# Moving the decay guard's loads and sums one expert block later in an RWKV and mixture-of-experts kernel

## The chip, the cores and the metric

The kernel runs on one core of one Trainium2 chip. The metric is the device time of one execution in microseconds (us); the time of a version is the median of several executions. The engines are named as in the profile: PE is TensorE (PEld its weight loads), DVE is VectorE, ACT is ScalarE, POOL is GpSimd, SP is the queue that issues most DMA transfers. "L483" is line 483 of the kernel before.

## What is computed

An RWKV attention (4 batches, 8 heads, 768 steps, head size 48) feeds a mixture of 8 experts with top-1 routing (3072 tokens of width 384, hidden width 1024).

```python
for t in range(S):                                   # attention, per batch and head
    cur = einsum('bhd,bhe->bhde', u[None] * kt, vt)
    y[:, :, t] = einsum('bhd,bhde->bhe', rt, state + cur)
    state = wt[:, :, :, None] * state + einsum('bhd,bhe->bhde', kt, vt)
logits = x @ w_gate + modality_bias[modality_id]     # x = y, one row of 384 per token
e_idx = argmax(logits); gate_w = softmax(logits)[e_idx]
for e in range(E):                                   # experts
    h = maximum(x[mask] @ w1[e], 0.0)
    out[mask] = gate_w[mask, None] * (h @ w2[e])
```

The kernel's fast attention is written for decays `w` between 0.78 and 1.25. A "decay guard" reads all of `w` once more and sums by how much any element lies outside; if the sum is not zero, a slow general path (`any_decay`) runs at the end.

## The kernel before, in words

The attention stage and the routing come first (to about 122 us). Rows of tokens are then scattered to DRAM by expert, and seven expert blocks follow, `seq` = 0 to 6, of 512, 512, 384, 384, 384, 512 and 416 rows (`WIDTH`). The schedule is written by hand: each engine executes in the order in which the program emits its instructions.

A block has two stages. The up stage "u" has 8 steps (`blk_up`): in each PE makes 9 matmuls into one PSUM tile (L792), ACT takes the ReLU to `hh` (L796), and DVE makes the remainder `hl` (L797). The down stage "d" goes over row chunks j of 128 rows (4 chunks in a block of 512 rows), 4 steps for each chunk (`blk_down`, L813, 6 matmuls a step), so step s belongs to chunk s // 4. A chunk's sum stands in PSUM tile pY for even j and in pX for odd j. After a chunk, `blk_out` lets ACT copy it out as `ot` (L834), and POOL sends it off (L835). Blocks 2 to 5 convert the next block's rows (`blk_t`: DVE L770 and L778, ACT L776) ahead of the down stage, and split the next block's first weights (`w_split`: ACT L276, DVE or POOL L277) in the four steps of chunk 0.

Extra work is hung on a step with `at(block, stage, step, fn)`. Several functions on one step run in the order in which they were registered. The ones that matter here:

- `guard_load(n)` (L476 to L478), n = 0 to 7: SP issues the load of one eighth of `w` (128 x 1152 f32, 0.59 MB) into a `wg` tile. There are two `wg` buffers, so load n waits for the sums of n - 2.
- `guard(n)` (L480 to L484): two ReLU activations on ACT over that tile, each with an accumulator that goes to its own column of `gacc`.
- `flags()` (L693 to L710), in two parts, registered after the guard (L1003 to L1005) on steps 7 and 9 of the down stage of block 5. Part one: DVE reduces all 16 columns of `gacc` (L697) and compares with zero into `gb` (L698). Part two: PE multiplies `gb` with ones (L701, one column), and DVE makes the four flags from it (L703 to L709).
- At the start of block 6 every engine's sequencer loads the flags (L1010), which decide over the extra paths after the last block.

In the kernel before, the guard's loads hang on up steps 2 and 6 of blocks 1 to 4, and its sums on down steps 4 and 7 of the same blocks. The tags "wg" also serve two tiles of block 6 (`ht`, `st`).

Of the kernel before, what the change touches and what calls it, by code (L numbers as in the profile page):

```python
# [55 lines left out]
NG = 8  # L56
# [17 lines left out]
def kernel(ctx: ExitStack, tc: tile.TileContext, rkw, vt, wf, cst, mid, wg, bias, w1, w2, out):  # L74
# [867 lines left out]
    seq = [*range(NQ)]  # L942
# [11 lines left out]
    def at(q, ph, step, *fn):  # L954
        aux.setdefault((q, ph, step), []).extend(fn)
# [36 lines left out]
        at(q1, "u", e // 2, part(pad_rows, e))  # L992
    at(q1, "u", 4, part(blk_raw, seq[2], 0))
    at(q1, "d", 0, part(blk_load, seq[2]))
    for k, q in enumerate(seq[1:1 + NG // 2]):
        for n, ph, step in ((2 * k, "u", 2), (2 * k + 1, "u", 6)):
            at(q, ph, step, part(guard_load, n))
        for n, step in ((2 * k, 4), (2 * k + 1, 7)):
            at(q, "d", step, part(guard, n))
# [223 lines left out]
```

## Time and profile before

| what | us |
|---|---|
| median of 3 executions (334.73 to 335.19) | 335.15 |
| the profiled execution, own time | 335.87 |
| span in the trace of that execution | 334.1 |
| PE busy in the span | 323.0 (97%) |
| ACT busy | 206.2 (62%) |
| DVE busy | 238.4 (71%) |
| POOL busy | 158.8 (48%) |

The time around the span (335.87 less 334.1) is start and end that the trace doesn't cover. In the trace the down stage of block 1 runs from about 174.5 to 191.2 us, block 4 ends at about 266.7, the up stage of block 5 goes to 283.5, its down stage to 300.4, and block 6 to about 328.3, after which the last rows are written out. Times in rows are from the start of the span.

### The profile page before, as it was taken

The numbers are of one execution on the slowest core, as the hardware profiler recorded it, in microseconds if no ns is written. First come the engines' busy times: TensorE is split into PE (matmuls) and PEld (weight loads), VectorE is DVE, ScalarE is ACT, GpSimd is POOL, SyncE is SP. The second block draws the span as 40 slices with busy tenths as digits, with TensorE's granted clock in tenths as the row PEclk, the third lists the DMA queues.
The fourth block names the chain that finished last, engine by engine and source line by source line (L and its number), as shares of the span: only waits on it lengthen the run. The fifth ranks groups of instructions, "written<-read, shape, count | busy, mean of one in ns | idle before, by whom it ended". The sixth has DMA issues, their size and how long they took to land.

```text
span 334.1 us, 10250 instructions
## 1 busy us (share of the span) xinstructions
PE 323.0 (97%) x3915; PEld 298.8 (89%) x3915; DVE 238.4 (71%) x510; ACT 206.2 (62%) x516; POOL 158.8 (48%) x194
## 2 busy tenths in 40 slices
PE   8989899999999999999999999999999999999993
PEld 3779899999898988899889999999999988999982
DVE  7899999999999886696458858858358445815510
ACT  2478388688879994461449556956956944614420
POOL 5889999999999179136751210210220220121021
PEclk9999799999999999999999999999999999999999
DMA  7998888888894601614964800440560663210001
GB/s 220 404 307 249 248 257 267 263 261 268 264 312 154 145 4 47 144 71 169 301 195 120 254 32 0 108 177 2 114 194 2 197 141 96 94 72 22 0 32 55
DMA packets 38735, 52.31 MB, mean 157 GB/s; under 512 B 19189, under 2 KB 26133, under 8 KB 38676
## 3 DMA queue, kind: packets, MB, share of 16 engines
q1 hardware_dynamic: 35572, 42.09, 42.9%
q0 software_dynamic: 3104, 9.47, 7.6%
q8 instruction: 33, 0.54, 0.7%
q14 instruction: 26, 0.21, 0.2%
HBM read 55.43 MB, written 11.88 MB: 202 GB/s over the span
## 4 chain that ended last, share of the span: by engine, by line
issue 40%; PE 20%; POOL 8%; POOLq 2%; ACT 1%; DVE 0%; ACTq 0%
PE pS_u L792 6%; POOL out L835 6%; PE pY_d L813 3%; PE pX_d L813 2%; POOL xs L724 2%; PE pY L466 2%; POOLq L1032 2%; PE pS L415 1%; PE pY L455 1%; PE pR_x L520 1%; PE pU L435 1%; PE pR_x L321 1%; ACT dV L356 0%; POOLq L835 0%; POOLq L1010 0%
## 5 line engine op out<-in xcount | busy, mean ns | idle before, releaser
L835 POOL DMA_INDIRECT out<-ot,xg x25 | 27.4, 1096 | 132.7 <-ACT ot L834 130.6
L797 DVE SCALAR_TENSOR_TENSOR hl<-pS_u,hh 128x512 fp32r<-128x512 f32 (+2 forms) x56 | 34.6, 619 | 62.5 <-ACT hh L796 62.3
L792 PE MATMUL pS_u<-xh,wh 128*128 128x512 f32 (+2 forms) x168 | 61.6, 367 | 0.0
L796 ACT ACTIVATE hh<-pS_u 128x512 fp32r<-128x512 f32 (+2 forms) x56 | 30.3, 541 | 50.5 <-PE pS_u L792 50.5
L792 PE MATMUL pS_u<-xh,wl 128*128 128x512 f32 (+2 forms) x168 | 61.3, 365 | 0.0
L277 DVE TENSOR_TENSOR wl<-raw,wh 128x768 fp32r<-128x768 f32 x52 | 48.8, 962 | 2.3 <-ACT wh L276 1.9
L276 ACT CAST wh<-raw 128x768 fp32r<-128x768 f32 (+1 forms) x60 | 44.9, 786 | 0.0
L792 PE MATMUL pS_u<-xo,wh 128*128 128x512 f32 (+2 forms) x168 | 43.3, 365 | 0.0
L813 PE MATMUL pY_d<-wh,hh 128*128 128x384 f32 x112 | 37.8, 337 | 0.0
L813 PE MATMUL pY_d<-wh,hl 128*128 128x384 f32 x112 | 37.6, 336 | 0.0
L813 PE MATMUL pY_d<-wl,hh 128*128 128x384 f32 x112 | 37.6, 336 | 0.0
L724 POOL DMA_INDIRECT xs<-xp,posT x24 | 26.4, 1101 | 21.7 <-DVE posT L607 17.8
L335 DVE TENSOR_TENSOR_SCAN pX_s<-pw,pX_s 128x268 f32<-128x268 f32 x48 | 34.1, 711 | 1.0 <-POOL pw L282 0.7
L792 PEld LDWEIGHTS pS_u<-xh,wh 128*128 128x128 f32 x168 | 31.5, 188 | 3.2
L792 PEld LDWEIGHTS pS_u<-xh,wl 128*128 128x128 f32 x168 | 31.5, 188 | 3.1
L792 PEld LDWEIGHTS pS_u<-xo,wh 128*128 128x128 f32 x168 | 31.0, 188 | 3.6 <-DVE xo L778 0.3
L287 POOL TENSOR_TENSOR G<-in 128x512 f32<-128x512 f32 x24 | 31.1, 1294 | 4.7 <-DMA in<-rkw 4.7
L417 DVE TENSOR_TENSOR A<-pS,cs 128x1024 f32<-128x1024 f32 x24 | 29.2, 1218 | 1.0 <-PE pS L415 1.0
L415 PE MATMUL pS<-R,K 64*128 64x128 f32 x384 | 27.7, 285 | 2.2 <-DVE A L417 1.4
L356 ACT ACTIVATE dV<-v,dT 128x48 f32<-128x48 f32 x120 | 29.7, 328 | 0.0
L299 POOL TENSOR_TENSOR in<-in 128x512 f32<-128x512 f32 (+1 forms) x23 | 28.1, 1223 | 0.6
L415 PEld LDWEIGHTS pS<-R,K 64*128 64x128 f32 x384 | 24.2, 194 | 3.7 <-DVE A L417 2.2
(319 smaller groups left out, 672.5 us busy)
## 6 DMA issues: line engine op xcount, KB each, us to landing
raw<-w SPq DMA_DIRECT2D x24, 768.0 KB
in<-rkw SPq DMA_DIRECT2D x66, 256.0 KB
v<-vt SPq DMA_DIRECT2D x24, 192.0 KB
wg<-wf SPq DMA_DIRECT2D x8, 576.0 KB
raw<-w SPq DMA_DIRECT2D x16, 192.0 KB
xs<-zt SPq DMA_DIRECT2D x12, 193.0 KB
xq<-xs SPq DMA_DIRECT2D x12, 192.0 KB
xq<-xs SPq DMA_DIRECT2D x12, 144.0 KB
```

The lines of the kernel that those rows point to most:

```text
L276: nc.scalar.copy(out=wh[k][:, sl], in_=raw[k][:, sl])
L277: (eng or (nc.vector, nc.gpsimd)[k]).tensor_tensor(out=wl[k][:, sl], in0=raw[k][:, sl], in1=wh[k][:, sl].bitcast(F32), op=ALU.subtract)
L287: nc.gpsimd.tensor_tensor(out=G, in0=t[:, 0:512], in1=t[:, 512:1024], op=ALU.mult)
L335: nc.vector.tensor_tensor_scan(out=BE[:, ::step], data0=pp[:, ::step], data1=d1[:, ::step], initial=0.0, op0=ALU.mult, op1=ALU.max)
L356: nc.scalar.activation(out=dV[:, h], in_=v0[:, h], func=AF.Copy, scale=dT[:, h:h + 1])
L415: nc.tensor.matmul(out=pS[:, hh, p], lhsT=K[q, p], rhs=R[q, p], start=True, stop=True)
L724: rows_apart("xs", nc.gpsimd.indirect_dma_start(out=xs[:, :], out_offset=bass.IndirectOffsetOnAxis(ap=posT[:, n:n + 1], axis=0), in_=T["xb ...
L792: nc.tensor.matmul(out=pp, lhsT=wsrc[0][:, g, c * P:(c + 1) * P], rhs=xsrc[:, c, 0:w], start=(n == 0), stop=(n == 3 * KC - 1))
L796: nc.scalar.activation(out=hh, in_=pp, func=AF.Relu)
L797: nc.vector.scalar_tensor_tensor(out=hl, in0=pp, scalar=0.0, in1=hh.bitcast(F32), op0=ALU.max, op1=ALU.subtract)
L813: nc.tensor.matmul(out=X["y", q, j][0:r1 - r0], lhsT=hsrc[:, r0:r1], rhs=wsrc[1][:, f], start=(f == 0 and n == 0), stop=(f == FC - 1 and n ...
L835: ins = nc.gpsimd.indirect_dma_start(out=out[:, :], out_offset=bass.IndirectOffsetOnAxis(ap=xg[0:m, j, 1:2].bitcast(I32), axis=0), in_=ot[ ...
```

## The change

The guard's pairs of loads and sums move one block later: parts 0 and 1 from block 1 to block 2, 2 and 3 from block 2 to 3, 4 and 5 from block 3 to 4, 6 and 7 from block 4 to 5. The steps inside the block, the order of the parts and everything else stay.

```diff
@@ -992,7 +992,7 @@
     at(q1, "u", 4, part(blk_raw, seq[2], 0))
     at(q1, "d", 0, part(blk_load, seq[2]))
-    for k, q in enumerate(seq[1:1 + NG // 2]):
+    for k, q in enumerate(seq[2:2 + NG // 2]):
         for n, ph, step in ((2 * k, "u", 2), (2 * k + 1, "u", 6)):
             at(q, ph, step, part(guard_load, n))
         for n, step in ((2 * k, 4), (2 * k + 1, 7)):
             at(q, "d", step, part(guard, n))
```

## Rows read from the trace of the kernel before

**Rows 1.** The page: PE's busy time, and its granted clock in 40 slices.
```profile
PE 323.0 (97%) x3915; PEld 298.8 (89%) x3915; DVE 238.4 (71%) x510; ACT 206.2 (62%) x516; POOL 158.8 (48%) x194
...
PEclk9999799999999999999999999999999999999999
```
**Rows 2.** Waits of PE, whole run: us in total, times, longest.
```profile
PE pS L415 <- DVE A L417: 1.4, 2, 1.3
...
PE pU L435 <- ACT KT L401: 0.2, 1, 0.2
```
**Rows 3.** Busy time by stage: length, PE, PEld, DVE, ACT, POOL, clock, DMA, GB/s.
```profile
157.00:174.50 17.50, 17.50 (x78) 14.26 (x77) 8.45 (x18) 7.66 (x12) 11.86 (x12) 1.00 0.81 260
174.50:191.20 16.70, 16.70 (x98) 16.66 (x97) 14.67 (x57) 11.88 (x19) 4.47 (x4) 1.00 0.63 169
...
266.60:283.50 16.90, 16.90 (x75) 13.66 (x74) 8.16 (x11) 8.30 (x15) 1.96 (x2) 1.00 0.53 131
283.50:300.40 16.90, 16.90 (x100) 16.70 (x99) 8.83 (x21) 6.71 (x11) 3.50 (x3) 1.00 0.23 82
```
**Rows 4.** Timeline of SP: start, us, line, transfer; guard loads and their neighbours.
```profile
160.46 0.35 SPq L478 DMA_DIRECT2D wg<-wf  x1
...
185.93 0.91 SPq L478 DMA_DIRECT2D wg<-wf  x2
...
267.52 2.51 SPq L758 DMA_DIRECT2D xg<-xs  x1
275.64 8.74 SPq L271 DMA_DIRECT2D raw<-w  x2
```
**Rows 5.** Timeline of ACT, down stage of block 4.
```profile
260.92 0.57 ACT L834 ACTIVATE ot<-pY_d,xg 128x384 f32<-128x384 f32 x1
261.39 1.25 ACT L483 ACTIVATE jk<-wg,glo 128x1152 bf16<-128x1152 f32 x1
...
266.69 0.18 ACT L484 ACTIVATION_READ_ACCUMULATOR jk<-wg,ghi 128x1 f32 x1
266.78 0.56 ACT L834 ACTIVATE ot<-pX_d,xg 128x384 f32<-128x384 f32 x1
```
**Rows 6.** Timeline of ACT, down stage of block 5.
```profile
287.11 3.03 ACT L276 CAST wh<-raw 128x768 fp32r<-128x768 f32 x4
290.05 0.57 ACT L834 ACTIVATE ot<-pY_d,xg 128x384 f32<-128x384 f32 x1
292.12 0.58 ACT L834 ACTIVATE ot<-pX_d,xg 128x384 f32<-128x384 f32 x1 [1.50 <-PE pX_d L813]
```
**Rows 7.** Timeline of DVE, down stage of block 5, first part of the flags.
```profile
291.50 0.17 DVE L697 TENSOR_REDUCE gsf<-gacc 128x1 f32<-128x16 f32 x1
291.70 0.16 DVE L698 TENSOR_SCALAR gbf<-gsf 128x1 bf16<-128x1 f32 x1
```
**Rows 8.** Timeline of PE, down stage of block 5, chunks 2 and 3.
```profile
294.01 0.18 PE L701 MATMUL pU_g<-gbf,onesb 128*128 128x1 bf16 x1
294.05 0.42 PE L813 MATMUL pY_d<-wh,hh 128*128 128x384 f32 x1
...
296.21 0.34 PE L813 MATMUL pX_d<-wh,hh 128*128 128x384 f32 x1
```
**Rows 9.** Chain that ended last: start, us, what; DVE hands over to PE.
```profile
89.91 0.48 DVE xp L490
...
90.43 0.88 PE pY L455 x16
```
**Rows 10.** Stretches with a fallen clock (columns as Rows 3).
```profile
36.00:38.00 2.00, 1.17 (x18) 1.08 (x19) 1.78 (x3) 0.00 (x0) 1.85 (x5) 0.67 0.93 267
38.00:40.00 2.00, 2.00 (x26) 2.00 (x28) 1.97 (x6) 0.97 (x2) 2.00 (x3) 0.50 0.68 213
```
**Rows 11.** Timeline of PE, two waits in the attention stage.
```profile
18.43 1.16 PE L415 MATMUL pS<-R,K 64*128 64x128 f32 x16 [1.25 <-DVE A L417]
...
36.83 1.10 PE L466 MATMUL pY<-v,A 128*64 128x48 f32 x16 [0.97 <-issue]
```

## The prediction

> **What bounds the kernel now.** I read the page first, then PE's waits, then the stretches by stage, then the timelines of ACT, DVE, SP and PE where the moved work leaves and where it arrives. The page has PE busy 97% of the span at a granted clock of nine tenths or more in every slice but one [rows 1]. The list of PE's waits holds seven lines; each names a matmul of the attention stage (the first and the last stand in [rows 2]), and none a matmul of the expert blocks (L792, L813). The stretches agree: PE is busy 17.50 of 17.50 us in the up stage of block 1, 16.70 of 16.70 in its down stage, and 16.90 of 16.90 in both stages of block 5 [rows 3]. So from about 122 us on the time is PE's own work, without a gap, and then a short tail in which the last rows are written. A move of work on other engines can give nothing there. It can only cost, if it makes PE wait; and what PE loses in block 5 nothing later gives back, because block 6 is gapless too.
>
> **What the change removes: block 1.** Two loads go from SP (issued at 160.46 and some 6 us later) and four activations from ACT. The nearest stretches bound the gain: PE already has 17.50 of 17.50 and 16.70 of 16.70 us there [rows 3], so it is 0, although DMA engines are busy 0.81 of the up stage and will be less so. The loss is 0 too: nothing is added there.
>
> **What stays as it was: blocks 2 to 4.** Each still has two loads and two guards on the same steps, only other eighths of `w`. SP runs ahead of the other engines: a pair that hangs on the up stage of block 2 is already issued at 185.93, in the down stage of block 1 [rows 4] (one of three such pairs). Its order against the other transfers in these blocks stays. Cost 0.
>
> **What the change adds: block 5, loads.** SP has the last transfer of block 6's rows at 267.52, which takes it 2.51 us, and its next one only at 275.64 [rows 4]. The two loads of parts 6 and 7 fall into this hole, at about 270. Their buffers are free by then, since the sums of parts 4 and 5 end in block 4 at 266.87 [rows 5]. They move 2 x 0.59 = 1.18 MB. At the mean of that stretch, 131 GB/s at a DMA share of 0.53 [rows 3], that takes 9.0 us, and at the same rate with the engines full 131 / 0.53 = 247 GB/s, 4.8 us. So the data is there between 275 and 279, more than 11 us ahead of its use at 290.5 (below). The second weights of block 6, which SP issues from 275.64 to 284.4, come up to 4 us later at worst; their first use is in the up stage of block 6, after 300.4. Cost of the loads 0; their cover is these 11 and 16 us.
>
> **Block 5, sums, and the wait that they make.** This is where it costs. In block 4 ACT copies out chunk 0 at 260.92, starts the first of the four activations 0.47 us later, and the last accumulator is read at 266.69 + 0.18 = 266.87 [rows 5], thus 5.95 us after the start of `ot`. The four run back to back, though they hang on steps 4 and 7: ACT has nothing between them. In block 5 ACT comes to the same `ot` at 290.05, late, because it has just cast weights from 287.11 on without a pause [rows 6]; nothing of that is touched by the change. With the guard behind it the last sum is written at 290.05 + 5.95 = 296.00.
>
> Part one of the flags hangs on step 7 of this same stage, behind guard part 7. Its reduction reads all 16 columns of `gacc`, so it now waits for 296.00; before, it ran at 291.50 without a wait, when the sums had been done since block 4. A hand-over between engines takes about 0.04 us, by DVE at 89.91 + 0.48 = 90.39 and PE at 90.43 [rows 9]; I take the same, as an estimate, for ACT to DVE, with 0 and 0.10 as ends. The two DVE instructions take 291.70 + 0.16 - 291.50 = 0.36 us [rows 7]. So `gb` is ready at 296.00 + 0.04 + 0.36 = 296.40, and PE may start the flags' matmul at 296.44. PE comes to it at 294.01 [rows 8]. It executes in order, and the rest of chunk 2, chunk 3 and block 6 are queued behind that one-column matmul. PE waits 296.44 - 294.01 = 2.43 us. DVE's own wait, from about 291.5 to 296.0, holds up only the flags: DVE has no other work until block 6's first `hl`.
>
> Two smaller things. After the wait the next matmul may have to show its weight load: 0 to 0.2 us. I take 0, because the matmul behind L701 follows it after 0.04 us now [rows 8]. And ACT's `ot` of chunk 1, now at 292.12, moves to 290.05 + (266.78 - 260.92) = 295.91 and ends 0.56 later, at 296.47. Chunk 3 writes the same PSUM tile, at 296.21 now [rows 6, 8]; by itself that would be a wait of 0.30 us. But PE, late by 2.43, comes to chunk 3 at 298.64, and the wait vanishes in the larger one. What is late next is the flags themselves: ready 2.4 us later, like all of PE's work, so the loads of the flags at block 6 keep their distance.
>
> **The sum.** 0 + 0 + 0 + 2.43 = 2.43 us, with ends 2.35 and 2.75 from the hand-overs and the weight load. For the profiled execution: span 334.1 + 2.4 = 336.5, own time 335.87 + 2.43 = 338.30. That execution is 0.72 us above the median of the runs shown, so for the median 335.15 + 2.43 = 337.58.
>
> **Rival 1: the clock falls in the wait as well.** In the attention stage PE waited 0.97 us before 36.83 [rows 11]; around it the granted clock went from 1.00 (2.4 GHz) to 0.50 (1.2 GHz) and stayed there until about 40: 0.67 as the mean of one stretch of 2 us (1.3 us at half), and 0.50 in the whole next one [rows 10], 3.3 us together. After a longer wait, 1.25 us before 18.43 [rows 11], the slice shows nine tenths or more [rows 1]. So a wait alone doesn't decide it; before both of them PE had run short, narrow matmuls with gaps, while in block 5 it runs wide ones without any. For the fall speaks that 2.43 us is twice the longest wait that this trace has. Its price: 3.3 us at half clock in a stage of gapless work loses up to 1.65 us; with the fall inside the wait a part of that is free. Time 337.58 + 1.65 = 339.23.
> The Trainium skill, page "TensorE: Matmul & The Clock Gate", section "HAM oscillation — how this bites in real kernels", says that a TensorE left idle too long between bursts is taken back to half clock and starts the next burst cold. By that rule this change pays twice for its wait, 339.2 in place of 337.6; the trace has one wait that agrees and one that doesn't, so it stays a rival with its own chance.
>
> **Rival 2, not slower: ACT is through in time.** One mechanism, in one place: if ACT reached chunk 0's `ot` in block 5 early enough, the sums would end before PE needs `gb`. The point: 294.01 - 0.44 - 5.95 = 287.62 in place of 290.05. Against it: until 290.05 ACT is in the weight casts that begin at 287.11 [rows 6], and the change takes no work from ACT in block 5. For it: only that the order could differ from what I read, or that the flags' reduction didn't wait for the last sums. The change would then not do what its step list says (the guard on step 7 ahead of the flags on step 7). Then the 0.30 us at chunk 3 is all that is left, or nothing: 335.15 to 335.45, no change that can be told.
>
> **Rival 3: the loads come late.** If parts 6 and 7 landed after 290.5, the wait would grow one for one. That needs a landing over 20 us after the issue; 1.18 MB need 4.8 to 9.0. I give it as 340 or more.
>
> **How the numbers follow.** Forecast (wait of 2.4 us, clock kept): 0.58, 337.6. Rival 1: 0.30, 339.2. Rival 2: 0.08, 335.15 to 335.45. Rival 3 and anything else: 0.04, half of it slower, half of it a gain that I don't see. A measurement of this kernel can tell about 0.2% (0.7 us) from no change. Faster by more: 0.02; within: 0.08; slower by more: 0.90. The range takes in the forecast with its ends (337.5 to 337.9, and 0.4 below for what the runs of before scatter, 334.73 to 335.19) and rival 1 with the same scatter: 337.1 to 339.5.
>
> **What would show it.** In the profile of the changed kernel PE's waits should hold one new line, the flags' matmul (L701) behind DVE L698, of about 2.4 us; DVE should wait for ACT L484 ahead of L697, some 4.5 us; ACT should run `ot`, four activations and the next `ot` without a pause from 290.05; the down stage of block 1 should be as long as now, 16.7 us. Rival 1 would show as a granted clock of 0.50 for some 3 us after the wait, with matmuls of chunk 2 or 3 twice as far apart. The prediction is wrong if L701 starts with no wait, if ACT pauses ahead of the first activation in block 5 (the loads were late), or if any stage of blocks 1 to 4 gets shorter by more than 0.1 us.

## The result, and the profile after

The changed kernel takes 338.94 us (median of 338.66 to 339.48) against 335.17 us before (334.73 to 335.43): 3.77 us more, ratio 1.0118 with a 95% interval of 1.0102 to 1.0134. The forecast was 337.6 in a range of 337.1 to 339.5. Executions more than 1.5% above the fastest of the same kernel are left out of ratios and counts; that is one, of the kernel before.

In the changed kernel's waits of PE there is one new line, and it is the first of them (columns as in [rows 2]):

```profile
PE pU_g L701 <- DVE gbf L698: 2.3, 1, 2.3
PE pS L415 <- DVE A L417: 2.1, 4, 1.3
```

The timeline of ACT in the down stage of block 5 answers [rows 5, 6]:

```profile
288.62 0.57 ACT L834 ACTIVATE ot<-pY_d,xg 128x384 f32<-128x384 f32 x1
289.10 1.24 ACT L483 ACTIVATE jk<-wg,glo 128x1152 bf16<-128x1152 f32 x1
...
294.38 0.19 ACT L484 ACTIVATION_READ_ACCUMULATOR jk<-wg,ghi 128x1 f32 x1
294.48 0.56 ACT L834 ACTIVATE ot<-pX_d,xg 128x384 f32<-128x384 f32 x1
```

and that of DVE [rows 7]:

```profile
294.60 0.17 DVE L697 TENSOR_REDUCE gsf<-gacc 128x1 f32<-128x16 f32 x1 [4.45 <-ACT jk L484]
294.81 0.16 DVE L698 TENSOR_SCALAR gbf<-gsf 128x1 bf16<-128x1 f32 x1
```

ACT copies out chunk 0, runs the four activations without a pause, and DVE stands 4.45 us ahead of L697 until the last sum is there. PE, from the flags' matmul to block 6 (answers [rows 8]):

```profile
295.02 0.18 PE L701 MATMUL pU_g<-gbf,onesb 128*128 128x1 bf16 x1 [2.28 <-DVE gbf L698]
295.06 0.42 PE L813 MATMUL pY_d<-wh,hh 128*128 128x384 f32 x1
...
296.44 0.52 PE L813 MATMUL pY_d<-wh,hh 128*128 128x384 f32 x1
296.76 0.52 PE L813 MATMUL pY_d<-wl,hh 128*128 128x384 f32 x1
...
300.00 0.33 PE L813 MATMUL pX_d<-wl,hh 128*128 128x384 f32 x1
300.17 0.34 PE L813 MATMUL pX_d<-wh,hl 128*128 128x384 f32 x1
...
302.95 0.35 PE L792 MATMUL pS_u<-xh,wh 128*128 128x416 f32 x1
```

The wait is read best against ACT's copy of chunk 0 (`ot`), whose place in the stage no kernel here changes: L701 started 294.01 - 290.05 = 3.96 us after it before [rows 6, 8], and 295.02 - 288.62 = 6.40 us now. PE lost 2.44 us. Then it lost more: between 296.4 and 299 the matmuls are 0.32 us apart, before and after that 0.17. The granted clock says why (columns as in [rows 3]):

```profile
295.50:296.00 0.50, 0.50 (x4) 0.50 (x4) 0.43 (x5) 0.00 (x0) 0.50 (x1) 0.87 0.00 0
296.00:296.50 0.50, 0.50 (x4) 0.50 (x3) 0.26 (x2) 0.00 (x0) 0.29 (x1) 0.50 0.00 0
...
299.00:299.50 0.50, 0.50 (x4) 0.50 (x4) 0.00 (x0) 0.18 (x1) 0.04 (x1) 0.72 0.00 0
299.50:300.00 0.50, 0.50 (x4) 0.50 (x3) 0.00 (x0) 0.00 (x0) 0.50 (x1) 1.00 0.07 16
```

It fell to 0.50 (1.2 GHz) at about 295.9, 0.9 us after PE had begun again, and rose at about 299.3. From L701 to block 6 PE took 302.95 - 295.02 = 7.93 us. A profile of the same kernel without the fall has 6.36 (below), and so has the kernel before, 300.37 - 294.01. The fall cost 1.57 us. Wait and fall together are 4.01 us: from the copy of chunk 0 to block 6 it was 300.37 - 290.05 = 10.32 in the trace of before, whose line is

```profile
300.37 0.35 PE L792 MATMUL pS_u<-xh,wh 128*128 128x416 f32 x1
```

and is 302.95 - 288.62 = 14.33 now.

The span grew by only 336.8 - 334.1 = 2.7. In the execution that was profiled before, the clock fell in the attention stage [rows 10]; in this one it did not. Its blocks begin 1.4 us earlier (L792 first at 120.4 in place of 121.8); 0.4 us of this was there ahead of the fall:

```profile
36.00:38.00 2.00, 2.00 (x52) 1.88 (x51) 1.77 (x6) 0.97 (x2) 1.85 (x5) 1.00 0.92 306
```

4.01 - 1.43 = 2.58, and 0.1 in block 6, make up the 2.7. The rest is as forecast. There is no gap in block 1 (stretches, columns as in [rows 3]):

```profile
157.00:174.50 17.50, 17.50 (x78) 14.31 (x78) 9.18 (x19) 8.02 (x14) 12.15 (x11) 1.00 0.49 176
174.50:191.20 16.70, 16.70 (x98) 16.70 (x97) 13.93 (x56) 6.49 (x11) 3.35 (x4) 1.00 0.66 190
```

From the start of block 1 to the down stage of block 5 PE took the same in both, 283.60 - 157.79 = 125.81 us in the trace of before,

```profile
157.79 0.39 PE L792 MATMUL pS_u<-xh,wh 128*128 128x512 f32 x1
...
283.60 0.33 PE L813 MATMUL pY_d<-wh,hh 128*128 128x384 f32 x1
```

and 282.18 - 156.37 = 125.81 in that of the changed kernel:

```profile
156.37 0.39 PE L792 MATMUL pS_u<-xh,wh 128*128 128x512 f32 x1
...
282.18 0.33 PE L813 MATMUL pY_d<-wh,hh 128*128 128x384 f32 x1
```

And in the timeline of SP the loads of parts 6 and 7 stand in its hole, 20 us ahead of their use [rows 4]:

```profile
268.78 0.85 SPq L478 DMA_DIRECT2D wg<-wf  x2
274.21 8.74 SPq L271 DMA_DIRECT2D raw<-w  x2
```

### The profile page after: what moved, and what is told of

It reads as the page before. It is cut to its first block, busy times and chain, and to the rows that moved or that the text cites. A ratio compares the mean times of both kernels' runs of the same rounds, so it can differ in the third digit from the quotient of the medians.

```text
span 336.8 us, 10250 instructions
## 1 busy us (share of the span) xinstructions
PE 323.9 (96%) x3915; PEld 299.2 (89%) x3915; DVE 238.2 (71%) x510; ACT 206.3 (61%) x516; POOL 158.9 (47%) x194
## 4 chain that ended last, share of the span: by engine, by line
issue 41%; PE 20%; POOL 8%; POOLq 2%; ACT 1%; DVE 0%; ACTq 0%
PE pS_u L792 6%; POOL out L835 6%; PE pY_d L813 3%; PE pX_d L813 2%; POOL xs L724 2%; PE pY L466 2%; POOLq L1032 2%; PE pS L415 1%; PE pY L455 1%; PE pR_x L520 1%; PE pU L435 1%; PE pR_x L321 1%; ACT dV L356 0%; POOLq L835 0%; POOLq L1010 0%
## 5 line engine op out<-in xcount | busy, mean ns | idle before, releaser
L792 PE MATMUL pS_u<-xh,wh 128*128 128x512 f32 (+2 forms) x168 | 61.6, 367 | 0.0
L792 PE MATMUL pS_u<-xh,wl 128*128 128x512 f32 (+2 forms) x168 | 61.3, 365 | 0.0
L792 PE MATMUL pS_u<-xo,wh 128*128 128x512 f32 (+2 forms) x168 | 43.3, 366 | 0.0
L792 PEld LDWEIGHTS pS_u<-xh,wl 128*128 128x128 f32 x168 | 31.5, 188 | 3.2
L792 PEld LDWEIGHTS pS_u<-xh,wh 128*128 128x128 f32 x168 | 31.5, 188 | 3.2
L792 PEld LDWEIGHTS pS_u<-xo,wh 128*128 128x128 f32 x168 | 31.0, 188 | 3.6 <-DVE xo L778 0.3
L813 PE MATMUL pX_d<-wh,hh 128*128 128x384 f32 x80 | 27.2, 340 | 0.0
```

The lines of the kernel that those rows point to most:

```text
L792: nc.tensor.matmul(out=pp, lhsT=wsrc[0][:, g, c * P:(c + 1) * P], rhs=xsrc[:, c, 0:w], start=(n == 0), stop=(n == 3 * KC - 1))
L813: nc.tensor.matmul(out=X["y", q, j][0:r1 - r0], lhsT=hsrc[:, r0:r1], rhs=wsrc[1][:, f], start=(f == 0 and n == 0), stop=(f == FC - 1 and n ...
```

## The experiments

They ran on three other chips, four kernels on each, beside the kernel before. The chip of the result is called A here, the others B, C and D. There the executions of the kernel before scatter more (335.4 to 337.5 on B) than on A (334.7 to 335.4), so the intervals are wide, and the timelines carry most of the argument. "Above before" is the difference of the medians; the ratio, to which the interval belongs, is not that of the medians (on C, 3.87 us above before go with a ratio of 1.0101, which is 3.4 us).

**Theory:** PE waits 2.44 us at the flags' matmul for the last sums, and in some executions the clock falls in that wait. **Rival A:** the loads and sums in block 5 themselves slow it. **Rival B:** the move costs something in blocks 1 to 4.

### The flags later

```diff
-    at(seq[-2], "d", 7, part(next, fl))
-    at(seq[-2], "d", 9, part(next, fl))
+    at(seq[-2], "d", 10, part(next, fl))
+    at(seq[-2], "d", 12, part(next, fl))
```

> The changed kernel, with the two parts of the flags moved from steps 7 and 9 to steps 10 and 12 of block 5's down stage; the guard stays in blocks 2 to 5. Theory (PE waits at the flags' matmul for the last sums, and the clock falls in that wait): no wait at L701, no fall, 335.2 to 335.5; of the wait of 0.30 us at the first matmul of chunk 3, behind ACT's copy of chunk 1, now something is seen. Rival A (the loads and sums themselves slow block 5, by traffic or a busy ACT): still 337 or more. Rival B (the parts of the move in blocks 1 to 4 cost something): 336 or more. A new cost is possible: the flags end some 3 us later, 1.5 us ahead of block 6, and the sequencers' loads of them could hold up PE there by up to 1 us.

Measured on B: 337.45 against 335.99, 1.46 above before, ratio 1.0037 (1.0020 to 1.0053). That is more than the theory's 0 to 0.3 us, less than the 1.8 or more of Rival A, and within the 0.8 or more of Rival B. In the timeline of PE L701 starts without a wait, and the hidden wait behind ACT's copy of chunk 1 stands where the prediction had it:

```profile
296.24 0.44 PE L813 MATMUL pX_d<-wh,hh 128*128 128x384 f32 x1 [0.29 <-ACT ot L834]
...
297.39 0.18 PE L701 MATMUL pU_g<-gbf,onesb 128*128 128x1 bf16 x1
...
300.46 0.34 PE L813 MATMUL pX_d<-wh,hl 128*128 128x384 f32 x1
300.74 0.43 PE L792 MATMUL pS_u<-xh,wh 128*128 128x416 f32 x1
```

At block 6 PE is 0.1 us late (0.28 from start to start, where 0.17 is usual). From ACT's copy of chunk 0 (289.76) to block 6 it took 300.74 - 289.76 = 10.98 us, 0.66 more than the 10.32 of before, in place of 4.01 more. So the guard in block 5 costs 0.66 us here once the flags don't wait, and Rival A has the smaller part. The timed 1.46 us is more than that. The up stage of block 6 takes 0.2 us longer than in the trace of before, and that of block 1 0.6 us (17.39 against 16.80), the subject of the last experiment.

### Only the last pair in block 5

```diff
-    for k, q in enumerate(seq[2:2 + NG // 2]):
+    for k, q in enumerate((*seq[1:NG // 2], seq[-2])):
```

> The changed kernel, but only the last pair of parts (6 and 7) is in block 5; the others are in blocks 1, 2 and 3 as before the change, and block 4 has none. Theory: the whole cost comes from the last pair, so the time is that of the changed kernel, 338.9, with a wait of 2.4 us at L701. Rival B (the move in blocks 1 to 4 costs or gains something): it differs from 338.9 by more than 0.5 us.

Measured on B: 339.31, 3.3 above before, ratio 1.0100 (1.0064 to 1.0137). The timeline of PE has the whole wait:

```profile
296.12 0.18 PE L701 MATMUL pU_g<-gbf,onesb 128*128 128x1 bf16 x1 [2.35 <-DVE gbf L698]
```

One of the four pairs brings the whole wait: from ACT's copy to block 6 it is 12.76 us, 2.44 more than before. Against Rival B. But the clock did not fall here, and the mean granted clock is 0.993 to 0.995 in all four executions. The 0.9 us that are left of the 3.3 are then not a fall in the wait.

### The flags' matmul one, two and minus one steps later

```diff
-    at(seq[-2], "d", 9, part(next, fl))
+    at(seq[-2], "d", 10, part(next, fl))
```

In the other two the new step is 11 and 8.

> The changed kernel, with the second part of the flags (the matmul on PE) on step 10 in place of 9. PE comes to it one step of 1.04 us later, so the wait is 2.44 - 1.04 = 1.40 us. Theory: 335.2 + 1.4 = 336.6 if the clock stays, 338.1 if it falls all the same; which of them, the theory leaves open. Rival A (the loads and sums themselves): no change from 338.9.

> The changed kernel, with the second part of the flags on step 11. PE comes two steps of 1.04 us later: the wait is 2.44 - 2.08 = 0.36 us, the same length as the wait for ACT's copy at the first matmul of chunk 3, which comes right behind and is then covered. Theory: 0.3 to 0.5 us above the kernel before, no fall of the clock. Rival A (the loads and sums in block 5 themselves cost the time): 2 us or more above it.

> The changed kernel, with the second part of the flags (the matmul on PE) on step 8 in place of 9. PE comes to it one step of 1.04 us earlier, so the wait is 2.44 + 1.04 = 3.48 us. Theory: 1.04 us slower than the changed kernel, and the clock, after the longer wait, falls in at least as many executions: 4.6 to 5.1 us above the kernel before. Rival (not the wait): as the changed kernel.

| step of L701, chip | wait of PE there, by the sum | idle in the trace | copy of chunk 0 to block 6, longer by | above before, us | ratio, interval |
|---|---|---|---|---|---|
| 11, D | 0.36 | 0.22 | 0.42 | 0.56 | 1.0022 (1.0007 to 1.0038) |
| 10, B | 1.40 | 1.26 | 1.41 | 1.64 | 1.0034 (1.0010 to 1.0057) |
| 9 (the change), A | 2.44 | 2.28 | 4.01, with a fall | 3.77 | 1.0118 (1.0102 to 1.0134) |
| 9 (the change), D | 2.44 | 2.29 | 2.45, no fall | 3.49 | 1.0124 (1.0096 to 1.0153) |
| 8, D | 3.48 | 3.32 | 6.01, with a fall | 5.62 | 1.0173 (1.0140 to 1.0205) |

The trace counts idle time from the modelled end of the matmul before, so it shows 0.16 us less than the starts do. Loads, sums and their places are the same in all these kernels; only PE's arrival moves. In each profile L701 starts 6.40 us after ACT's copy of chunk 0 (6.41 in that with step 11): the sums are ready at one time, and PE waits for as long as it comes too early. The time follows it; for the longer two it rises by more than the wait. With step 8 it lies outside the 4.6 to 5.1 us expected: 2.13 us above the changed kernel beside it in place of 1.04. The timeline of PE in the kernel with step 8 shows the other part:

```profile
297.63 0.18 PE L701 MATMUL pU_g<-gbf,onesb 128*128 128x1 bf16 x1 [3.32 <-DVE gbf L698]
...
298.14 0.52 PE L813 MATMUL pY_d<-wl,hh 128*128 128x384 f32 x1
298.46 0.52 PE L813 MATMUL pY_d<-wh,hl 128*128 128x384 f32 x1
```

and so do its stretches (columns as in [rows 3]):

```profile
295.00:297.00 2.00, 0.00 (x0) 0.00 (x0) 0.00 (x0) 1.97 (x4) 0.00 (x0) 0.84 0.00 0
297.00:299.00 2.00, 1.37 (x5) 1.37 (x6) 1.25 (x9) 0.65 (x3) 0.98 (x1) 0.50 0.00 0
299.00:301.00 2.00, 2.00 (x7) 2.00 (x7) 0.00 (x0) 0.00 (x0) 0.00 (x0) 0.50 0.27 98
301.00:303.00 2.00, 2.00 (x8) 2.00 (x8) 0.00 (x0) 0.00 (x0) 0.00 (x0) 0.50 0.01 4
303.00:305.00 2.00, 2.00 (x13) 2.00 (x12) 0.00 (x0) 0.58 (x1) 0.54 (x1) 0.96 0.01 4
```

Here the clock falls while PE still waits, and stays at 0.50 until 303.2, twice as long as in the changed kernel on A.

### The wait filled

```diff
     pG = pt("g", "pU")
+    for _ in range(10):
+        nc.tensor.matmul(out=pG[:, 0:C_D], lhsT=wm[:, 0:P], rhs=wm[:, 0:C_D], start=True, stop=True)
```

> The changed kernel, with ten matmuls of 504 bf16 columns that nobody uses put on PE directly ahead of the flags' matmul, in the place where it waits; they need about 2.1 us at full clock and the rest of the wait, 0.3 us, stays. Theory (wait 2.44 us, plus a clock that falls because PE stands still): the wait is filled, not shortened, so PE loses the same 2.4 to 2.5 us, but the clock stays at 1.00, and the time is 337.6. Rival (what goes beyond 2.4 us is not the clock): 338.9, as the changed kernel.

> The kernel with ten unused matmuls in the place of the wait, again, now beside the changed kernel on the same chip. Theory: PE loses the same 2.44 us at the flags' matmul, but never stands still for long, so the clock doesn't fall there: 2.4 to 2.6 us above the kernel before. If the clock is what the changed kernel loses beyond 2.44, the fill makes it faster than the changed kernel, by up to 1.5 us (by 1.5 times the share of executions in which the clock falls there). Rival (it isn't the clock): both take the same.

> The changed kernel beside it. Theory: 2.44 us of wait, and 1.5 us more in those executions in which the clock falls in the wait: 3.0 to 4.0 us above the kernel before, with mean granted clocks of 0.985 to 0.990 in the slower executions. Rival: mean clocks as in the kernel before, and a time as the fill.

Measured: on B 339.03, 3.04 above before, ratio 1.0080 (1.0053 to 1.0108), between the theory's 2.4 and the 3.8 of its rival. On D, beside the changed kernel: the fill 339.75, 2.58 above before, 1.0090 (1.0069 to 1.0111); the changed kernel 340.66, 3.49 above, 1.0124 (1.0096 to 1.0153). The timeline of PE with the fill on D (L702 is the fill; the lines below it are two further down than before):

```profile
295.00 2.30 PE L702 MATMUL pU_g<-wm 128*128 128x504 bf16 x10
297.45 0.16 PE L703 MATMUL pU_g<-gbf,onesb 128*128 128x1 bf16 x1
...
303.80 0.35 PE L794 MATMUL pS_u<-xh,wh 128*128 128x416 f32 x1
```

L703 again comes 6.40 us after ACT's copy (291.05), and block 6 follows 6.35 us behind it, at full clock. So the fill neither shortens nor lengthens what PE loses to the flags. The changed kernel took 0.91 us more than the fill in the medians; the intervals overlap, so that useless work is cheaper than standing still is likely here and not shown. The mean granted clock of each execution goes the same way: 0.990 or less in 10 of 16 executions of the changed kernel on the three chips where it was timed (3 of 4, 4 of 6, 3 of 6), in none of the 10 with the fill, and in 5 of 74 of the kernel before on the other chips. It is only a hint and not a count of falls in the wait. The clock also falls in the attention stage in some executions, and behind the last matmul in every profile. None of the 4 executions with only the last pair in block 5 has so low a mean, with the same wait. And the executions of the changed kernel with the low mean are slower than its others by only 0.2, 0.5 and 1.2 us on A, C and D (means), not by 1.57.

In two further profiles of the changed kernel the clock did not fall in or behind the wait. One of them, on C, is the reference for the 6.36 us above:

```profile
296.29 0.18 PE L701 MATMUL pU_g<-gbf,onesb 128*128 128x1 bf16 x1 [2.29 <-DVE gbf L698]
302.65 0.35 PE L792 MATMUL pS_u<-xh,wh 128*128 128x416 f32 x1
```

That one and the same wait has a fall behind it in one execution and none in another is seen in the attention stage too. The wait of 1.25 us before 18.43 [rows 11], which had none, is in all 14 profiles of this case (1.22 to 1.26 us). In seven of them the clock fell, 1.5 to 2.1 us after PE had begun again; the kernel before, profiled again on C, is one (timeline of PE, then stretches with columns as in [rows 3]):

```profile
18.10 1.16 PE L415 MATMUL pS<-R,K 64*128 64x128 f32 x16 [1.26 <-DVE A L417]
```

```profile
20.00:22.00 2.00, 2.00 (x41) 2.00 (x38) 1.97 (x4) 1.90 (x9) 1.55 (x2) 0.56 0.85 251
22.00:24.00 2.00, 2.00 (x40) 1.91 (x40) 1.89 (x5) 1.07 (x5) 1.21 (x4) 0.59 0.91 259
```

### Block 1: both kernels again, and both without the last pair

In the profiles of the first four experiments PE waits 0.3 or 1.1 us in the up stage of block 1. Four more kernels ask whether the change does that: the two kernels themselves, and both without parts 6 and 7 of the guard (loads and sums left out, the reduction reads 12 columns), parts 0 to 5 in blocks 2 to 4 or in blocks 1 to 3.

```diff
-    for k, q in enumerate(seq[2:2 + NG // 2]):
+    for k, q in enumerate(seq[2:1 + NG // 2]):
```

is the moved one, and the other has, in the place of the same line,

```diff
+    for k, q in enumerate(seq[1:NG // 2]):
```

> The kernel before, profiled beside the others on the chip of the experiments. In three of the first four profiles ACT's ReLUs come late in the up stage of block 1, at about 164 to 168 us, by 0.3 to 2 us, and PE waits 0.3 or 1.15 us there; neither the kernel before nor the changed one shows that in its first trace. If this lateness belongs to the chip and not to the change, the same is seen here, with 0 to 1.2 us of wait in block 1. If it comes from the change (code or transfers that now lie otherwise), PE has no wait here in block 1.

> The changed kernel on the same chip. Theory: 2.44 us of wait at L701, so 2.4 more than the kernel before beside it if the clock keeps up in most executions, 3.9 if it falls in most. Rival B (blocks 1 to 4 cost something too): a wait in block 1 that the kernel before doesn't have, up to 1.2 us on top.

> The changed kernel without parts 6 and 7 of the guard (their loads and sums are left out, the reduction reads 12 columns): parts 0 to 5 in blocks 2, 3 and 4, nothing in block 5. Theory: no wait at L701, and the time of the kernel before, within 0.3 us. Rival B: slower than the next kernel by 0.5 to 1.5 us, because of block 1.

> The kernel before without parts 6 and 7: parts 0 to 5 in blocks 1, 2 and 3. Theory: the time of the kernel before, within 0.3 us, and the same as the run before this one. Rival B: faster than that run by 0.5 to 1.5 us.

Measured on C: the kernel before 336.19, ratio 0.9992 (0.9970 to 1.0015) to its other executions there (335.92); the changed kernel 339.79, 3.87 above, 1.0101 (1.0068 to 1.0134); moved without the last pair 337.07, 1.15 above, 1.0015 (0.9994 to 1.0036); not moved without it 337.03, 1.11 above, 1.0027 (1.0005 to 1.0049). The kernel before has the wait in block 1 too, in the timeline of PE of this profile:

```profile
168.94 0.50 PE L792 MATMUL pS_u<-xh,wh 128*128 128x512 f32 x1 [1.11 <-DVE hl L797]
```

It comes from ACT, whose timeline there is:

```profile
161.56 0.60 ACT L796 ACTIVATE hh<-pS_u 128x512 fp32r<-128x512 f32 x1 [0.78 <-issue]
163.95 0.60 ACT L796 ACTIVATE hh<-pS_u 128x512 fp32r<-128x512 f32 x1 [1.79 <-PE pS_u L792]
...
167.56 1.08 ACT L796 ACTIVATE hh<-pS_u 128x512 fp32r<-128x512 f32 x2 [2.29 <-remote]
```

Its ReLUs, 2.1 us apart in the trace of before on A, come late there, and PE waits. The wait is in every profile from these chips, 0.3 to 1.9 us long, with and without guard work in block 1, so the change is not needed for it. The up stage of block 1 took 16.8 us in both profiles on A and 17.4 to 19.0 in the others.

Moved or not moved makes 0.04 us between the two kernels without the last pair, with an interval of some 0.7 us either way by the scatter of their 12 executions each. That alone would leave room for the smallest cost that Rival B allows, 0.5 us. The two profiles on A close most of it: block 1 to the down stage of block 5 takes 125.81 us in both.

Both kernels without the last pair missed their expectation of 0.3 us: they lie some 1 us above the kernel before by the medians (0.5 and 0.9 by the ratios), though they do less. In their traces there is no wait at L701, and from ACT's copy to block 6 they take 10.32 and 10.27 us, no longer than before. Two differences are seen elsewhere: the time from PE's last matmul to the end of the span is 5.9 to 6.1 us, against 5.5 to 5.9 in the other twelve profiles, and the up stage of block 1 took 18.84 us in the moved one, 17.41 in the other, 18.18 in the kernel before on C. What makes them so, and whether that is the whole excess, isn't explained.

## Why the prediction was right or wrong

- **Blocks 1 to 4 cost and give nothing.** Right: 125.81 us from block 1 to the down stage of block 5 in both profiles on A, and 0.04 us between moved and not moved.
- **The loads.** Right: issued at 268.78 where "about 270" was said, and ACT does not pause for them.
- **The sums.** Right: 5.95 us from ACT's copy to the last accumulator in the sum; 294.38 + 0.19 - 288.62 = 5.95 in the trace.
- **The wait at L701.** Right in place and size: 2.43 predicted, 2.44 measured. Four positions of the matmul moved it by one step each, as it should.
- **The wait of 0.30 us at chunk 3, hidden behind the larger one.** Right in place: 0.29 of idle when the flags were moved out of the way. PE lost a little more, 0.46 us by the starts of the matmuls (296.24, where 295.78 would have followed on).
- **The clock.** Here the central forecast was off. It held that the clock keeps up (0.58) and gave the fall 0.30. The profiled execution had the fall: 2.44 + 1.57 us. The range held because it was drawn over both cases, with rival 1 at 339.2, and not because the choice between them did; the measured 338.94 is nearer to rival 1 than to 337.6. For the choice between the two cases there was little to go by: the prediction weighed two waits of one execution, of 0.97 and 1.25 us, of which one went with a fall, and the second has a fall behind it in half of the profiles. How often the clock falls at L701 stays open: it did in one of four profiles with this wait, and by the hint of the mean clock in 10 of 16 executions of the changed kernel. As an estimate, 2.44 + 10/16 x 1.57 = 3.4 us, where 3.77, 3.87 and 3.49 were measured; some of what is measured on B, C and D is the unexplained excess of the last experiment and not the clock.
- **The price of the fall.** Predicted up to 1.65, measured 1.57 in the one profile of the changed kernel that has it. The prediction let the fall begin inside the wait; there it began 0.9 us after it.
- **The page's rule.** The Trainium skill, page "TensorE: Matmul & The Clock Gate", section "HAM oscillation — how this bites in real kernels", lets an idle stretch that is too long end in a cold start. The profile with the wait of 3.48 us agrees: L701 already starts at 0.50. That of 2.44 us on A agrees in its cost, but PE started at 1.00 there and fell later, and three further profiles with this wait (the two of the changed kernel, and the one with only the last pair in block 5) have no fall. The idle stretches of which the page speaks are longer than the wait forecast here, so the prediction's "by that rule" asked more of the page than it states.

What stays open: how often the clock falls behind a wait of this length, what makes ACT late in block 1 on the chips of the experiments, and why the kernels without the last pair were 1 us above the kernel before.

## What to carry to other kernels

Before moving work on an engine with slack, list who reads its last result, and compare the time at which that reader stands in its own queue with the time at which the moved work ends; here a small check held up PE, the one engine that had no time to spare. What stood behind a small waiting instruction waited with it: one column of matmul cost PE 2.44 us. And where a stretch of PE without a gap gets a wait of some us, budget the clock beside the wait, as a cost that comes in some executions. Before anything else, try to place the waiting instruction later: two steps further on nearly all of the cost was gone (0.56 us left).

## What the runs showed of the hardware

- The clock can fall after PE has resumed: in the changed kernel on A at about 295.9, 0.9 us behind the end of the wait, with dense matmuls running. It was back at 299.3.
- Of four profiles with the wait of 2.44 us, in nearly the same program, one has a fall behind it and three have none; the wait of 3.48 us had one for twice as long (296.4 to 303.2). Of the 14 profiles with a wait of 1.25 us in the attention stage, seven have a fall behind it.
- A matmul of 384 columns follows the next at 0.32 us at a granted clock of 0.50 and at 0.17 at 1.00, so a little more than half the rate is left at half the clock.
- In block 1, in every profile from B, C and D and in neither from A, ACT's ReLUs came late and PE waited 0.3 to 1.9 us.
